# A linear-attention scan and its feed-forward on one Trainium2 core: the last eight chunks' feed-forward in pairs, two chunks' transposes back on TensorE

## The chip, the cores and the metric

The kernel runs on one core of a Trainium2 chip. The core has five engines that run beside each other and wait for one another by semaphores: TensorE (PE; its weight loads are shown as PEld), VectorE (DVE), ScalarE (ACT), GpSimd (POOL) and SyncE (SP), whose queue issues nearly all DMA transfers here. The metric is the device time of one execution in microseconds (us).

## What is computed

The first part is a recurrence per batch and head over 768 tokens, with a state of 48 x 48; the second is a feed-forward on all 3072 tokens.

```
# r, k, v, w: (4, 8, 768, 48);  u: (8, 48)
for t in range(768):
    y[t]  = r[t] @ (state + outer(u * k[t], v[t]))
    state = w[t][:, None] * state + outer(k[t], v[t])
x   = y of all heads side by side        # (3072, 384)
h   = x @ w_in                           # (384, 2048)
out = maximum(0.01 * h, h) @ w_out       # (2048, 384), float32
```

## The kernel before

**Chunks.** The 3072 tokens are cut into 24 chunks of 128 (six to a batch entry). Chunks 0 to 3 are handled in two interleaved pairs (`pair`, line 491), chunks 4 to 23 one by one (`single`, line 668). For a chunk, w, k, r and v are loaded by four DMAs (line 470; 192-byte pieces in single chunks). ACT takes the logarithm of w (line 332), PE makes the running sum over tokens with a triangular matrix (cp, line 691), ACT's exponentials (line 342) and DVE's products (line 348) make the scaled r and k, both in the tile rk. rk has to be transposed to rkT (`turn`, line 376) for the score matmuls (line 750); DVE masks the scores (line 412); PE sums state part and score part into yp (lines 780 and 785); DVE adds the bonus term and leaves y (line 444). y is transposed into xT, which holds the feed-forward's input of all tokens (`finish`, line 439). PE, DVE and POOL carry the state to the next chunk (lines 761, 434 and 421).

**Two ways to transpose.** For the chunks in `TDMA` (line 150), one DMA transpose on SP's queue makes rkT (line 381) and one makes the chunk's columns of xT (line 450). For the others, PE does eight 128 x 128 transposes of rk into the PSUM banks se and so (line 391), which DVE (line 399) and ACT (line 401) copy to rkT, and three of y into the bank yp (line 458), which ACT copies to xT (line 465). `TDMA` begins at chunk 12.

**Feed-forward.** `blocks` (line 158) says how many chunks make a block: one each. The up-projection of a block (line 821) goes in items: an item fills one PSUM bank hp of 512 columns, which with a block of one chunk are four tiles of d_ff by 128 tokens, three matmuls each (384 = 3 x 128), so 12 matmuls of 128 columns. A Prelu on ACT (line 855) takes the bank to g. The down-projection goes per chunk in four items of four matmuls of 384 columns into a bank op (line 873); the sum is copied out by ACT (line 885) or, from chunk 14 on, DVE (line 889), and an SP DMA writes it (line 893). There are two hp banks, two op banks and three g tiles. The up items of block n are interleaved in proportion with the down items of block n - 1 (lines 834 to 845), and each up item depends on the xT of all chunks of its block:

```
m1.append((up, j, J, N, g, chs, [xt_steps[ch] for ch in chs] + win_s[j * 128 // 512]))
```

**Order.** No instruction is issued while the steps are described. Each step names its engine, a guessed duration, its dependences and a priority; `Plan.order` (line 37) simulates the engines with these guesses and emits every engine's instructions in the simulated order of start. Each engine then runs its queue strictly in that order, waiting where it has to. Priorities: scan steps by chunk (10 per chunk), feed-forward items behind all of them (1000 and up), Prelu and output copies ahead (5 and 3). A DMA's guessed share of the transfer time is its `wire`: `WIRE` (line 155) for each of a single chunk's four loads, 1.7 for an rkT transpose, 0.65 for an xT transpose; transfers queue one behind the other in the simulation. Two limits keep the scan from running far ahead: the loads of chunk n depend on the running sum of chunk n - 5 (`AHEAD`), and the logarithm of chunk n on the first up item of chunk n - 8 (`LEAD`, line 899).

Of the kernel before, what the change touches and what calls it, by code (L numbers as in the profile page):

```python
# [123 lines left out]
def kernel(  # L124
# [15 lines left out]
    NCH = B * C  # L140
# [6 lines left out]
    NQ = FF // 512  # L147
    OACT = 14
    NCI = 3
    TDMA = range(12, NCH)  # L150
    LEAD = 8
    AHEAD = 5

    PAIRS = (0, 2)
    PWIRE, WIRE = 1.45, 1.15
    WEIGHTS = [(2, 20.15)] + [(4, 24.0)] * 7
    CASTS = 3
    blocks = [1] * NCH
    assert sum(blocks) == NCH

    pool = ctx.enter_context(tc.tile_pool(name="pool", bufs=1))
# [49 lines left out]
    with tc.manual_schedule():  # L211
# [51 lines left out]
        def step(eng, dur, fn, pri, reads=(), writes=(), deps=(), wire=None, rows=0):  # L263

            d = list(deps)
            for x in writes:
                d += x.old
            i = plan.add(eng, dur, fn, d, pri, wire, rows)
            for x in (*reads, *writes):
                x.steps.append(i)  # L270
            return i
# [104 lines left out]
        def turn(rk, rkT, s_d, n, P0, banks):  # L376

            if n in TDMA:
                return [step(
# [59 lines left out]
        def finish(yp, vs, s_y, s_vs, n, P0):  # L439
# [6 lines left out]
            col = n * L  # L446
            if n in TDMA:
                xt_steps.append(step(
# [483 lines left out]
```

## Time and profile before

| | us |
|---|---|
| time, median of 3 runs (lowest to highest) | 188.97 (188.82 to 189.43) |
| the profiled execution: its time | 188.97 |
| its span, first to last instruction | 187.3 |
| PE busy | 174.0 |
| DVE, ACT, POOL busy | 128.0, 116.3, 108.7 |
| PE: 1152 up matmuls (line 821), mean of one | 0.219 |
| PE: 384 down matmuls (line 873), mean of one | 0.326 |
| ACT: 96 Prelus of 512 columns (line 855), mean of one | 0.597 |
| DMA transpose to rkT (12), to xT (12), median to landing | 3.5, 2.6 |
| one single-chunk load of 192 KB, median to landing | 3.6 to 3.9 |

The span is shorter than the time; the difference lies around the first and last instruction. Matmuls overlap in the array, so a matmul's own duration (0.219 us) is longer than the distance from its start to the next one's; for what PE can do in a time, the distance of starts counts. "Idle before" an engine's instruction is the time in which the engine did nothing, and the profile names whose semaphore ended it. The DMA rows give the share of the core's 16 DMA engines.

### The profile page before, as it was taken

The page shows a single profiled execution, that of the slowest core. Times are in us where ns is not written, and L with a number is a line of the kernel's source. Part 1 is how long each engine was busy: PE and PEld are TensorE (multiplying, and loading weights), DVE is VectorE, ACT ScalarE, POOL GpSimd, SP SyncE. Part 2 cuts the span into 40 slices and gives each one's busy share as a digit, 9 for nine tenths or more (in the row PEclk, how much of TensorE's full clock was granted, in tenths as well). Part 3 has the DMA queues.
Part 4 walks back from the last instruction along what each step waited for, and adds up shares of the span by engine and source line. Part 5 has one row for each costly group of instructions (what it writes and reads, how often), then busy time and mean ns, then how long its engine had stood idle before and what let it go on. Part 6 is the DMA issues. An engine that isn't in the chain of part 4 may idle for free.

```text
span 187.3 us, 6219 instructions
## 1 busy us (share of the span) xinstructions
PE 174.0 (93%) x2550; PEld 136.1 (73%) x2550; DVE 128.0 (68%) x226; ACT 116.3 (62%) x254; POOL 108.7 (58%) x148
## 2 busy tenths in 40 slices
PE   3678579999999999999999999999999999999992
PEld 1255567688778878788787787878887877877871
DVE  2399784887789787877967999766876856441111
ACT  2646586678876877796687666676374645334430
POOL 7799922175899898978792885170545755400000
PEclk9999999999999999999999999999999999999999
DMA  5999999889899997987899879997789996512102
GB/s 147 261 316 322 385 370 302 156 189 217 164 221 211 185 221 158 221 193 172 174 207 190 156 155 229 119 200 141 159 180 179 191 202 142 123 44 67 38 7 84
DMA packets 116383, 34.62 MB, mean 185 GB/s; under 512 B 109697, under 2 KB 114818, under 8 KB 116354
## 3 DMA queue, kind: packets, MB, share of 16 engines
q1 hardware_dynamic: 116352, 34.22, 82.9%
q8 instruction: 20, 0.33, 0.7%
q14 instruction: 9, 0.07, 0.1%
q10 hardware_dynamic: 2, 0.00, 0.0%
HBM read 25.17 MB, written 4.72 MB: 160 GB/s over the span
## 4 chain that ended last, share of the span: by engine, by line
PE 81%; SPq 7%; DMA 6%; issue 1%; POOL 1%; DVE 1%; POOLq 0%; DVEq 0%
PE op L873 33%; PE hp L821 32%; DMA in<-in_moe_w_out_dram 6%; SPq L470 4%; PE se L750 3%; SPq L290 3%; PE yp L785 2%; PE cp L691 2%; PE yp L761 2%; PE yp L780 1%; PE so L391 1%; PE se L391 1%; PE yp L458 1%; PE cp L696 1%; PE yp L654 1%
## 5 line engine op out<-in xcount | busy, mean ns | idle before, releaser
L855 ACT ACTIVATE g<-hp 128x512 bf16<-128x512 f32 x96 | 57.1, 597 | 42.3 <-PE hp L821 41.4
L821 PE MATMUL hp<-xT,w_in_b 128*128 128x128 bf16 x1152 | 79.0, 219 | 0.3 <-DVE rkT L399 0.3
L873 PE MATMUL op<-w_out_b,g 128*128 128x384 bf16 x384 | 76.5, 326 | 0.8 <-DVE w_out_b L313 0.8
L821 PEld LDWEIGHTS <-w_in_b 128*128 128x128 bf16 x1152 | 69.3, 98 | 7.2 <-DVE w_in_b L313 0.2
L873 PEld LDWEIGHTS <-g 128*128 128x128 bf16 x384 | 33.0, 97 | 15.6 <-issue 0.9
L357 POOL TENSOR_TENSOR ru<-in,ub 128x384 f32<-128x384 f32 x24 | 26.9, 1119 | 19.7 <-DMA in<-in_r_dram 19.7
L369 POOL TENSOR_TENSOR vs<-in,dg 128x384 f32<-128x384 f32 x24 | 20.2, 843 | 14.7 <-DVE dg L365 11.0
L361 POOL TENSOR_TENSOR ru<-ru,in 128x384 f32<-128x384 f32 x24 | 25.7, 1072 | 0.9
L348 DVE TENSOR_TENSOR rk<-in,er 128x384 bf16<-128x384 f32 x24 | 18.2, 757 | 7.4 <-DMA in<-in_r_dram 5.5
L348 DVE TENSOR_TENSOR rk<-in,ek 128x384 bf16<-128x384 f32 x24 | 22.0, 919 | 1.4 <-ACT a L738 0.9
L421 POOL TENSOR_TENSOR sb<-s,a 128x384 bf16<-128x384 f32 x17 | 16.1, 947 | 10.7 <-DVE s L434 10.1
L412 DVE TENSOR_TENSOR m<-se,maskb 128x512 bf16<-128x512 f32 x20 | 13.8, 689 | 7.3 <-PE so L750 7.1
L444 DVE TENSOR_TENSOR y<-yp,vs 128x384 bf16<-128x384 f32 x24 | 13.3, 553 | 7.5 <-PE yp L785 5.1
L889 DVE COPY o<-op 128x384 f32<-128x384 f32 x10 | 5.6, 558 | 18.2 <-PE op L873 18.1
L337 POOL CAST vb<-in 128x384 bf16<-128x384 f32 x24 | 14.6, 614 | 4.5 <-DMA in<-in_v_dram 4.5
L332 ACT ACTIVATE lw<-in 128x384 bf16<-128x384 f32 x24 | 12.4, 520 | 3.9 <-DMA in<-in_w_dram 3.8
L365 DVE TENSOR_REDUCE dg<-ru 128x8 f32<-128x384 f32 x24 | 13.0, 543 | 1.9 <-POOL ru L361 1.8
L412 DVE TENSOR_TENSOR m<-so,maskb 128x512 bf16<-128x512 f32 x20 | 13.6, 680 | 0.0
L342 ACT ACTIVATE er<-cp 128x384 f32<-128x384 f32 x22 | 10.8, 492 | 3.5 <-DVE ci L716 3.0
L716 DVE TENSOR_TENSOR ci<-cp,lw 128x384 f32<-128x384 f32 x20 | 11.0, 549 | 1.8 <-ACT g L855 0.9
L342 ACT ACTIVATE ek<-ci 128x384 f32<-128x384 f32 x20 | 10.5, 526 | 0.0
L391 PEld LDWEIGHTS <-rk 128*128 128x128 bf16 x96 | 6.7, 103 | 5.0 <-DVE rk L348 4.2
(103 smaller groups left out, 191.0 us busy)
## 6 DMA issues: line engine op xcount, KB each, us to landing
out_dram<-o SPq DMA_DIRECT2D x24, 192.0 KB, 2.5
in<-in_w_dram SPq DMA_DIRECT2D x20, 192.0 KB, 3.6
in<-in_k_dram SPq DMA_DIRECT2D x20, 192.0 KB, 3.8
in<-in_r_dram SPq DMA_DIRECT2D x20, 192.0 KB, 3.9
in<-in_v_dram SPq DMA_DIRECT2D x20, 192.0 KB, 3.8
in<-in_moe_w_in_dram SPq DMA_DIRECT2D x4, 768.0 KB, 8.5
in<-in_moe_w_out_dram SPq DMA_DIRECT2D x4, 768.0 KB, 12.6
in<-in_w_dram SPq DMA_DIRECT2D x2, 384.0 KB, 5.0
```

The lines of the kernel that those rows point to most:

```text
L337: "POOL", 0.57, lambda: nc.gpsimd.tensor_copy(out=vb.t[:], in_=vn.t),
L342: "ACT", 0.5, lambda: nc.scalar.activation(out=out.t[:], in_=i, func=AF.Exp, scale=scale),
L348: lambda: nc.vector.tensor_tensor(out=rk.t[:, a, :, 0:D], in0=xn.t, in1=e.t[:], op=ALU.mult),
L357: lambda: nc.gpsimd.tensor_tensor(out=ru.t[:], in0=rn.t, in1=ubv, op=ALU.mult),
L361: lambda: nc.gpsimd.tensor_tensor(out=ru.t[:], in0=ru.t[:], in1=kn.t, op=ALU.mult),
L369: lambda: nc.gpsimd.tensor_tensor(out=vs.t[:], in0=vn.t, in1=dg.t[:].unsqueeze(2).to_broadcast([128, H, D]), op=ALU.mult),
L412: lambda par=par: nc.vector.tensor_tensor(out=m.t[:, par], in0=gt(sc[par].t), in1=mask.unsqueeze(1).to_broadcast([128, NP, 128]), op=ALU.m ...
L421: lambda: nc.gpsimd.tensor_tensor(out=sb.t[:].rearrange("p g a d -> p (g a) d"), in0=s_in.t[:].rearrange("p g a d -> p (g a) d"), in1=a_ap ...
L444: lambda: nc.vector.tensor_tensor(out=y.t[:], in0=hd(yp.t[:, 0:DM]), in1=vs.t[:], op=ALU.add),
L821: nc.tensor.matmul(hp.t[:, a * N : (a + 1) * N], lhsT=w_in_b[:, t, (j + a) * 128 : (j + a + 1) * 128], rhs=xT[:, t, c0 : c0 + N], start=(a ...
L855: lambda hp=hp, g=g, j=j, J=J, N=N: nc.scalar.activation(out=g.t[:, j : j + J, 0:N], in_=hp.t[:, 0 : J * N].rearrange("p (a n) -> p a n", ...
L873: nc.tensor.matmul(op.t[:, 0:DM], lhsT=g.t[:, j, off : off + 128], rhs=w_out_b[:, j, :], start=(j == 0), stop=(j == NJ - 1))
```

## The change

Chunks 12 and 13 are taken out of `TDMA`, so their rk and y are transposed on PE and copied by DVE and ACT as those of the chunks before; DMA transposes begin with chunk 14. The last eight chunks' feed-forward is done in four blocks of two chunks: an up item then fills its hp bank with two d_ff tiles by 256 tokens, six matmuls of 256 columns. A block has eight up items and eight down items. All g tiles become twice as wide (`max(blocks) * L`). The planner's guess for a single-chunk load goes from 1.15 to 1.18.

```diff
-    TDMA = range(12, NCH)
+    TDMA = range(14, NCH)
     LEAD = 8
     AHEAD = 5
 
     PAIRS = (0, 2)
-    PWIRE, WIRE = 1.45, 1.15
+    PWIRE, WIRE = 1.45, 1.18
     WEIGHTS = [(2, 20.15)] + [(4, 24.0)] * 7
     CASTS = 3
-    blocks = [1] * NCH
+    blocks = [1] * 16 + [2] * 4
```

## The prediction

> **What bounds the kernel now.** I first read the page's busy shares and slices.
>
> ```profile
> PE 174.0 (93%) x2550; PEld 136.1 (73%) x2550; DVE 128.0 (68%) x226; ACT 116.3 (62%) x254; POOL 108.7 (58%) x148
> ...
> PE   3678579999999999999999999999999999999992
> ...
> PEclk9999999999999999999999999999999999999999
> DMA  5999999889899997987899879997789996512102
> ```
>
> TensorE (PE) is full in every slice (4.7 us each) from the seventh to the last but one, at full granted clock; its idle time lies in the first 28 us. The DMA engines are nearly as full up to the 33rd slice, so two suspects remain. To choose between them I ask for the windows (length, then busy time of PE, PEld, DVE, ACT and POOL, clock, DMA share):
>
> ```profile
> 27.00:130.00 103.00, 102.69 (x1577) 82.08 (x1577) 81.46 (x140) 75.79 (x173) 69.40 (x78) 1.00 0.94 192
> 130.00:180.00 50.00, 49.94 (x682) 39.87 (x679) 26.89 (x46) 24.68 (x51) 18.21 (x21) 1.00 0.60 129
> ```
>
> and for the waits of PE from 27.3 us to the end, which hold a single row, ended at 27.31:
>
> ```profile
> PE op L873 <- DVE w_out_b L313: 0.8, 1, 0.8
> ```
>
> A busy PE may hide small gaps under overlapping matmuls, so I also took the starts of consecutive matmuls: the largest delay beyond the usual pitch after 27.3 us, apart from the changes between 128-row and 48-row matmuls, is 0.23 us at 144.4. From 27.3 to the last matmul PE is one dense queue; the time is startup, plus the sum of PE's pitches, plus the tail (copy of 0.56 us and the last output, 183.9 to 187.3). DMA is busy but late for nobody on PE. So I price the change in pitches.
>
> **What the change adds to PE.** Chunks 12 and 13 get their transposes back on PE: 8 of rk (line 391) and 3 of y (line 458) each. A chunk that has them now (start, duration, instruction):
>
> ```profile
> 79.20 0.39 PE L391 MATMUL se<-ident,rk 128*128 128x128 bf16 x4
> 79.42 0.39 PE L391 MATMUL so<-ident,rk 128*128 128x128 bf16 x4
> 79.65 0.83 PE L821 MATMUL hp<-xT,w_in_b 128*128 128x128 bf16 x12
> 80.32 0.33 PE L458 MATMUL yp<-ident,y 128*128 128x128 bf16 x3
> 80.48 0.81 PE L873 MATMUL op<-w_out_b,g 128*128 128x384 bf16 x4
> ```
>
> Durations overlap; what counts is start to start: 79.20 to 79.65 is 0.45 for eight, 80.32 to 80.48 is 0.165 for three. Two chunks: 2 x (0.45 + 0.165) = **+1.23 us**. They stand in a full queue, so nothing hides them.
>
> A rule of the Trainium skill prices them higher, so row and rule are weighed. The row: 22 transposes at a pitch of 56 ns, at granted clock 1.00; the groups' mean of 227 ns is one transpose's own duration, which overlaps the next. "TensorE: Matmul & The Clock Gate", Part 4, puts a PE transpose at about 275 ns in a kernel's context and says that full clock does not engage for it. At 275 ns the 22 would be an estimated 6 us; the pitch of the trace is used.
>
> **What it takes from PE.** The up-projections of chunks 16 to 23 are now 8 x 48 = 384 matmuls of 128 columns; they become 192 of 256. An item of 12 starts at 79.65 and its successor at 80.32: 0.67, so 55.8 ns each. The down-projection's four of 384 columns take 0.65, so 162.5 each. The line through the two gives 109.2 ns for 256 columns. An item, now 6 matmuls, goes from 0.670 to 0.655, and 32 items save **0.47 us**. The trace has no matmul of 256 columns, so bounds: two of 128, 111.6 (saving nothing), and one of 384 less one of 128, 106.7 (192 x 4.9 ns = 0.94 us). I take the line, because the small matmuls lie near it too (96 columns 42.5, 48 columns 25).
>
> The same page's section "Back-to-back issue gap" speaks of 81 ns at 128 columns and 131 at 512 in a stream with weight loads. Interpolated (98 at 256) that would be an estimated 12 us saved. The trace has its 128-column matmuls, each with its own weight load, at 55.8 ns, so that gain isn't there to take.
>
> Net on PE: 1.23 - 0.47 = **+0.76**, bounds +0.29 to +1.23.
>
> **What moves off the path.** SP loses four DMA transposes (lines 381 and 450: 3.5 and 2.6 us to landing by median, 1.2 to 1.9 us each on SP's queue between 92 and 111 us). The loads, outputs and transposes queued behind them there come sooner. Their 256-byte packets are a sixth of the queue's packet time: 25.2 us of all 16 engines for 24 transposes, so 4.2 us for these four. PE waits for none of it now, so the gain is nothing by itself; it is time gained for the scan of the later chunks. ACT gets two rkT copies of 0.59 and two xT copies of 0.48 (2.1 us), DVE two copies of 0.42. They lie in 90 to 115 us, where ACT is 65 to 75% and DVE 80 to 87% busy; their cover is the lead of xT over the up-projection, below. Without cover the full 3.0 us could show. POOL is untouched. The transposes bring waits to PE's queue: for DVE's rk products and for y, with ups and downs queued behind; ten chunks pay them now, and after 27.3 us all of these together left 0.2 us (one wait of the weight load of line 391 for rk). For two more chunks I take nothing; above, 0.2 us.
>
> ACT's Prelu keeps 96 instructions of 512 elements (0.60). Ups and downs alternate one to one in both versions except where a pair's 8 ups follow a single chunk's 4 downs: 8 x 0.655 + 4 x 0.65 of PE, plus scan work, against 8 x 0.60 of ACT, which fits. The last PE work, DVE's copy and the output DMA keep their sizes, so the tail stays.
>
> WIRE (1.15 to 1.18) changes the planner's guess for single-chunk loads only. The first of these, chunk 4's, issues at 22.43 us behind all weight loads, so the startup before it is planned as now. From there the four engine queues may be ordered anew; at the median this costs nothing, because PE finds ready work whichever comes first. Bounds: 1.7 us of gaps at 23.7 to 27.3 that might fill, and the lead of chunk 4's xT, only 0.5 us, that might be lost.
>
> **The wait that the change adds.** A pair's first up now needs the second chunk's xT as well. I counted up items (four of 12 to a chunk) and set their start beside xT's issue on SP:
>
> ```profile
> 131.69 2.25 SPq L450 DMA_TRANSPOSE xT<-y  x1
> ...
> 168.73 1.74 SPq L450 DMA_TRANSPOSE xT<-y  x1
> ```
>
> These are chunks 17 and 23. With 2.6 us to landing they arrive at 134.3 and 171.3 (their own landings: 133.9 and 171.6). Chunk 16's ups start at 132.93 and chunk 22's at 170.53: 1.0 too early for a pair, each time. Chunks 19 and 21 land 4.5 us before and level with the ups of 18 and 20. On PE, behind a waiting up stand downs and the whole scan; ACT and DVE follow. Against a stall: PE reaches these ups about 1 us later after the change, the scan gains up to 4.2 us of DMA time, and downs of the block before can go first (0.65 us each, if the planner sees the lateness). So I price it at nothing in the forecast. Uncovered it costs 1.0 + 1.0 = 2.1 us.
>
> **The sum.** The profiled execution took 188.97 us with a span of 187.3 (1.7 around it), and is itself the median of the three runs. 188.97 + 0.76 = **189.7 us**; a measurement tells about 0.3% (0.57 us) from no change, so "slower" begins at 189.54.
>
> **Rivals.**
> - The pair starves. If the planner's picture of the DMA is rosier than the chip, the first up of (16,17) and of (22,23) sits at the head of PE's queue until xT lands: up to 2.1 us more, 191.8; half of it, 190.8. It decides from the point where chunk 17 lands less than one item before the ups of 16. For it: the 1.0 us deficits. Against it: the DMA time freed, a whole chunk's worth.
> - The width buys nothing: a 256-column matmul costs two of 128, and only the transposes show: 190.2. Against it: four column counts on one line.
> - The startup gaps fill (the other side). If the new order from 22.4 us puts ready ups into the gaps at 23.7 to 27.3, up to 1.7 us come back: 189.7 - 1.7 = 188.0; half of it, 188.9. It decides only if over 0.76 us is filled. Against it: the last gap ends with the w_out cast after its landing at 26.4, which no WIRE moves.
> - Relief of the DMA shortens the whole. For it: DMA shares of 0.9 and over. Against it: PE's empty list of waits. Its price is at most PE's 0.23 us gap, so no case of its own.
>
> **Chances.** Forecast 0.57 (its own range, from the net's bounds, 189.3 to 190.2), starving pair 0.18, no gain from width 0.10, filled gaps 0.15. Faster than 188.40: over half of the filled gaps, 0.09. Within 0.3%: the rest of that and a third of the forecast, 0.06 + 0.19 = 0.25. Slower: 0.66. For 8 in 10 I leave out the fuller half of the gaps and the worst starving: 188.8 to 191.2.
>
> **What would show it.** Right: line 391 with 16 more and 458 with 6 more transposes on PE, four starts 0.22 apart; 192 up matmuls of 256 columns, an item of six 0.655 after its start; PE's waits after 27.3 us still nearly empty; the last matmul some 0.8 us later; xT of 17 and 23 earlier by 2 to 4 us. Wrong: a PE wait of over 0.3 us ahead of line 821 from 130 us on, ended by a landing; six wide matmuls in 0.67 or more, or under 0.64; a first down-projection well before or after 27.3; or a PE that ends earlier though its pitches sum to more.

## The result

Before: 188.91 us, the median of 6 runs (188.65 to 189.43). Changed: 190.11 us, the median of 6 (189.98 to 190.61). The ratio is 1.0061, with a 95% interval of 1.0042 to 1.0081: slower by 0.8 to 1.5 us. The forecast was 189.7 with a range of 188.8 to 191.2, and "slower" at 0.66. The profiled execution of the changed kernel took 189.99 us with a span of 188.2; against the 188.97 and 187.3 of before that is 1.02 and 0.9 more. In the experiments the runs of the kernel before, made beside them on the same chip, spread from 188.5 to 192 us, so a ratio there is known only to 0.3 or 0.4%; where less matters, the profiles decide.

The page's busy line and slices of the changed kernel:

```profile
PE 177.1 (94%) x2380; PEld 136.9 (73%) x2380; DVE 126.7 (67%) x228; ACT 118.4 (63%) x258; POOL 107.8 (57%) x148
...
PE   3688899999999999999999999999999999999992
...
PEclk9999999999999999999999999999999999999999
DMA  6999999988988999977988999869997773121112
```

TensorE is as full as it was. The slices of DMA are emptier in the fourth quarter, where the transfers ended earlier, and the time didn't follow them. The busy 177.1 is no measure of the change: in this execution the matmuls before 25.6 us ran at half their rate (12 ups from 23.37 to 24.65, 1.28 us and not 0.67), waiting for weights anyway, so they filled idle time. The windows from 27 us on (length, then PE, PEld, DVE, ACT, POOL, clock, DMA share):

```profile
27.00:130.00 103.00, 102.57 (x1583) 82.11 (x1581) 82.34 (x145) 77.35 (x175) 71.64 (x82) 1.00 0.91 190
130.00:180.00 50.00, 50.00 (x506) 37.77 (x504) 25.19 (x44) 25.88 (x54) 15.03 (x18) 1.00 0.54 113
```

and PE's waits from 27.3 us on:

```profile
PE op L873 <- DVE w_out_b L313: 0.2, 1, 0.2
PE so L391 <- DVE rk L348: 0.2, 1, 0.2
```

There is one new row, the wait of a transpose for rk, and none for xT ahead of line 821. The queue is still dense, so its length can be taken apart by starts. I measured each profile from the first down-projection matmul to the last matmul:

| kernel | first down | last matmul | between them | span |
|---|---|---|---|---|
| before | 27.31 | 183.53 | 156.23 | 187.3 |
| changed | 27.28 | 184.35 | 157.07 | 188.2 |

Of the 1.02 us between the two profiled executions, 0.84 lies between these two matmuls, -0.03 before them, 0.08 in the tail and 0.13 outside the span.

### The profile page after: what moved, and what is told of

It is laid out like the page before. It is cut to its first block, busy times and chain, and to the rows that moved or that the text cites. A ratio compares the mean times of both kernels' runs of the same rounds, so it can differ in the third digit from the quotient of the medians.

```text
span 188.2 us, 5870 instructions
## 1 busy us (share of the span) xinstructions
PE 177.1 (94%) x2380; PEld 136.9 (73%) x2380; DVE 126.7 (67%) x228; ACT 118.4 (63%) x258; POOL 107.8 (57%) x148
## 4 chain that ended last, share of the span: by engine, by line
PE 77%; SPq 8%; DMA 8%; DVE 2%; ACT 1%; issue 1%; ACTq 0%
PE op L873 31%; PE hp L821 31%; DMA in<-in_moe_w_out_dram 6%; SPq L470 5%; PE se L750 3%; SPq L290 3%; DMA in<-in_w_dram 2%; PE yp L785 2%; PE cp L691 2%; PE yp L761 2%; PE yp L780 1%; DVE rk L348 1%; PE so L391 1%; PE se L391 1%; PE yp L458 1%
## 5 line engine op out<-in xcount | busy, mean ns | idle before, releaser
L821 PE MATMUL hp<-xT,w_in_b 128*128 128x128 bf16 (+1 forms) x960 | 79.8, 233 | 0.0
L821 PEld LDWEIGHTS <-w_in_b 128*128 128x128 bf16 x960 | 65.4, 99 | 7.8
L873 PEld LDWEIGHTS <-g 128*128 128x128 bf16 x384 | 34.3, 98 | 16.0 <-issue 0.5
L357 POOL TENSOR_TENSOR ru<-in,ub 128x384 f32<-128x384 f32 x24 | 25.9, 1078 | 10.8 <-DMA in<-in_r_dram 10.8
L361 POOL TENSOR_TENSOR ru<-ru,in 128x384 f32<-128x384 f32 x24 | 24.7, 1029 | 1.1
L348 DVE TENSOR_TENSOR rk<-in,ek 128x384 bf16<-128x384 f32 x24 | 20.8, 868 | 1.4 <-ACT ek L342 1.3
L337 POOL CAST vb<-in 128x384 bf16<-128x384 f32 x24 | 15.6, 653 | 2.5 <-DMA in<-in_v_dram 2.5
L391 PEld LDWEIGHTS <-rk 128*128 128x128 bf16 x112 | 8.2, 107 | 4.9 <-DVE rk L348 4.3
```

The costliest lines, as they stand in the source:

```text
L337: "POOL", 0.57, lambda: nc.gpsimd.tensor_copy(out=vb.t[:], in_=vn.t),
L348: lambda: nc.vector.tensor_tensor(out=rk.t[:, a, :, 0:D], in0=xn.t, in1=e.t[:], op=ALU.mult),
L357: lambda: nc.gpsimd.tensor_tensor(out=ru.t[:], in0=rn.t, in1=ubv, op=ALU.mult),
L361: lambda: nc.gpsimd.tensor_tensor(out=ru.t[:], in0=ru.t[:], in1=kn.t, op=ALU.mult),
L821: nc.tensor.matmul(hp.t[:, a * N : (a + 1) * N], lhsT=w_in_b[:, t, (j + a) * 128 : (j + a + 1) * 128], rhs=xT[:, t, c0 : c0 + N], start=(a ...
L873: nc.tensor.matmul(op.t[:, 0:DM], lhsT=g.t[:, j, off : off + 128], rhs=w_out_b[:, j, :], start=(j == 0), stop=(j == NJ - 1))
```

## The experiments

Each kernel was executed 6 to 12 times, beside the kernel before. The table gives the timed result and the same stretch of PE's queue; the texts on record and the reading follow.

| run | median, us | ratio to before [95%] | stretch, us | against 156.23 |
|---|---|---|---|---|
| e1 transposes only | 190.55 | 1.0041 [1.0008, 1.0074] | 157.25 | +1.02 |
| e2 pairs only | 188.66 | 0.9958 [0.9924, 0.9992] | 155.48 | -0.75 |
| e3 WIRE only | 189.33 | 1.0001 [0.9968, 1.0034] | 156.38 | +0.15 |
| e4 change, WIRE 1.15 | 191.41 | 1.0098 [1.0064, 1.0131] | 158.04 | +1.81 |
| e6 no rkT transposes | 188.86 | 0.9988 [0.9967, 1.0008] | 156.22 | -0.01 |
| e7 six pairs | 191.86 | 1.0129 [1.0087, 1.0171] | 159.29 | +3.06 |
| e8 pairs, DMA from 11 | 189.19 | 0.9997 [0.9968, 1.0026] | 155.59 | -0.64 |
| e9 doubled again | 190.55 | 1.0039 [1.0001, 1.0076] | 157.30 | +1.07 |
| e10 pairs, WIRE 1.18 | 189.63 | 0.9982 [0.9948, 1.0017] | 155.92 | -0.31 |
| e11 change, WIRE 1.21 | 189.96 | 1.0021 [0.9987, 1.0056] | 157.04 | +0.81 |
| e12 change again | 190.16 | 1.0027 [0.9995, 1.0059] | 156.98 | +0.75 |

The run e5 stands with e9. The theory was that of the prediction: from 27.3 us on TensorE's queue is dense and the time is the sum of its pitches. The rivals were that the pairs starve, that freed DMA time counts, and that the new order of the queues makes the difference.

### The parts alone: e1, e2, e3, e4

```diff
 e1:  TDMA = range(14, NCH)
 e2:  blocks = [1] * 16 + [2] * 4
 e3:  PWIRE, WIRE = 1.45, 1.18
 e4:  TDMA = range(14, NCH);  blocks = [1] * 16 + [2] * 4   # WIRE stays 1.15
```

> Only the transposes of chunks 12 and 13 go back to TensorE; blocks stay at one chunk, WIRE stays 1.15. Theory of the dense queue (the time is startup plus the sum of TensorE's start-to-start pitches plus tail): 22 transposes more, 188.9 + 1.23 = 190.1 us, and TensorE's waits after 27.3 us stay under 0.5 us. Rival, the DMA time set free is worth something by itself: under 189.5. Rival, the loss of the change comes from the pairs' wait for xT: 188.9, since there are no pairs here.

> Only the last eight chunks' feed-forward in pairs; DMA transposes from chunk 12, WIRE 1.15. Theory of the dense queue: 32 items at 0.655 in place of 0.670, 188.9 - 0.47 = 188.4 us if the planner fills the time until the second chunk's xT with other work. Rival, the pair starves without the DMA time that the full change frees: waits of TensorE ahead of the first up item of chunks 16 and 22 of about 1.0 us each, 188.4 + 2.1 = 190.5. Rival, the wide matmul saves nothing: 188.9.

> Only the planner's guess for a single-chunk load goes from 1.15 to 1.18: the same work in another order. Theory of the dense queue: 188.9 us, within 0.3. Rival, the new order of the queues carries the part of the loss that the pitches don't explain: 189.2 to 189.5.

> The whole change but for the planner's guess, which stays 1.15. Theory of the dense queue: as the whole change, 188.9 + 0.76 = 189.7 by the pitches (the whole change measured 190.1). Rival, the order set by 1.18 costs 0.4 us: 189.7 here against 190.1 there. Rival, the order set by 1.18 is what keeps the pairs supplied: waits of over 0.5 us ahead of a pair's first up, 190.6 or more.

The transposes alone cost, with no pair in the kernel; so the loss isn't the pairs' wait, and the four DMA transposes less bring nothing back. In e1's profile the pitches after lines 391 and 458 sum to 6.48 us where before has 5.25: the 1.23 of the forecast. The 0.2 less in the stretch lies in small gaps, which differ from order to order and, as e9 shows below, from one execution to the next.

The pairs alone gain 0.53 us by the medians beside each other (0.15 to 1.4 by the interval), where 0.47 was expected, and they do so with the DMA as loaded as before. Their stretch is 0.75 shorter, more than the pitches give, because two gaps of before's profile (0.23 and 0.16) are absent and only one of 0.20 is new. Six wide matmuls take an item's time as forecast; in the changed kernel (start, duration, instruction):

```profile
172.79 0.82 PE L821 MATMUL hp<-xT,w_in_b 128*128 128x256 bf16 x6
173.44 0.81 PE L873 MATMUL op<-w_out_b,g 128*128 128x384 bf16 x4
174.09 0.82 PE L821 MATMUL hp<-xT,w_in_b 128*128 128x256 bf16 x6
174.75 0.33 PE L873 MATMUL op<-w_out_b,g 128*128 128x384 bf16 x1
```

From 172.79 to 173.44 is 0.65, and the pitch of one is 109 ns. WIRE alone changes nothing that can be measured. But in e4, with the old WIRE, the change is 1.3 us slower still than as it was made (0.97 of it in the stretch). Its PE queue ahead of the first pair, the 48-row score matmuls left out:

```profile
137.35 0.82 PE L873 MATMUL op<-w_out_b,g 128*128 128x384 bf16 x4
138.01 0.36 PE L785 MATMUL yp<-vb,m 128*128 128x48 bf16 x8
138.71 0.32 PE L691 MATMUL cp<-lw,trev 128*128 128x384 bf16 x1 [0.33 <-ACT a L738]
...
139.29 0.33 PE L761 MATMUL yp<-vb,rk 128*128 128x96 bf16 x4 [0.18 <-DVE y L444]
...
140.35 0.33 PE L780 MATMUL yp<-sb,rkT 128*128 128x96 bf16 x4
140.51 0.36 PE L785 MATMUL yp<-vb,m 128*128 128x48 bf16 x8
140.72 1.47 PE L821 MATMUL hp<-xT,w_in_b 128*128 128x256 bf16 x12
```

The downs of chunk 15 have run out at 138.0; until the pair's first up at 140.72 only scan steps are left, each waiting for another engine. Four gaps of 0.49, 0.32, 0.28 and 0.24 us add up to 1.33. The waits carry the names of ACT and DVE, but what is missing is ready feed-forward work: chunk 17's xT landed at 139.5. The last two gaps, 0.5 us, come after that landing; there the pair's ups were ready but stood behind scan steps in the queue, so that part is the order's and not the DMA's. The same stretch of the changed kernel has a down directly ahead of the pair:

```profile
133.59 0.83 PE L821 MATMUL hp<-xT,w_in_b 128*128 128x128 bf16 x12
134.26 0.81 PE L873 MATMUL op<-w_out_b,g 128*128 128x384 bf16 x4
134.91 0.33 PE L761 MATMUL yp<-vb,rk 128*128 128x96 bf16 x4
135.08 0.81 PE L873 MATMUL op<-w_out_b,g 128*128 128x384 bf16 x4
135.73 1.47 PE L821 MATMUL hp<-xT,w_in_b 128*128 128x256 bf16 x12
```

### The price of a transpose with the order held: e5, e9

```diff
-                    for g in range(NP):
+                    for g in [*range(NP)] * (2 if n in (8, 9) else 1):
...
-                for g in range(KT):
+                for g in [*range(KT)] * (2 if n in (8, 9) else 1):
```

> The kernel before, with each of the 22 TensorE transposes of chunks 8 and 9 issued twice into the same place. The planner's durations are untouched, so the order of every engine is that of before, no DMA is freed and the results stay the same. Theory of the dense queue: 22 pitches more, +1.23 us, 190.2 against 188.97. Rival, the transposes find slack in TensorE's queue and the loss of the change has another cause: within 0.3 of before. Rival, a transpose on TensorE costs its whole 0.23 us: +5.

> The same kernel as in the run with doubled transposes, whose profile was taken at a granted clock of 0.68 and so can't be read against before: every engine's order as in the kernel before, 22 transposes of chunks 8 and 9 issued twice. Theory of the dense queue: from the first down-projection to the last matmul 156.2 + 1.2 = 157.5 us, and 190.2 in all. Rival, slack in the queue: 156.2 and 189.0. Rival, more than the pitch is paid (a transpose holds the queue beyond 56 ns): 158 or more.

e5 came out at 1.0113 [1.0068, 1.0159] of before from four of its six executions; the profiled one took 256.87 us at a granted clock of 0.68, which makes every pitch longer, so it says slower and no more. e9 settles it by its profile. There the pitches after lines 391 and 458 sum to 6.48 us where before has 5.25, +1.23. The stretch is 1.07 longer, because two gaps of before's profile, 0.23 at 144.4 and 0.16 at 53.0, aren't there and one of 0.24 ahead of 31.4 is new. As the order is the same in both, gaps of this size come and go between executions. A chunk with its transposes doubled:

```profile
65.61 0.61 PE L391 MATMUL se<-ident,rk 128*128 128x128 bf16 x8
66.06 0.81 PE L873 MATMUL op<-w_out_b,g 128*128 128x384 bf16 x4
66.71 0.61 PE L391 MATMUL so<-ident,rk 128*128 128x128 bf16 x8
67.16 0.33 PE L458 MATMUL yp<-ident,y 128*128 128x128 bf16 x3
```

Eight take 0.45, not eight times 0.23. Same order, no DMA moved, no wide matmul: 22 transposes cost 1.23 us of queue. In e9 no copy on ACT or DVE is added, in e1 four of rkT and two of xT are, and their stretches are alike (157.30 and 157.25): the copies cost nothing that shows.

### Freed DMA time alone: e6

```diff
         def turn(rk, rkT, s_d, n, P0, banks):
+            if n in (12, 13):
+                return list(s_d)
```

> The kernel before, leaving out the rkT transposes of chunks 12 and 13 altogether, on DMA and on TensorE: their scores and state parts are computed from what an earlier chunk left in the tile. Two of the four DMA transposes that the change removes are gone, 3.1 of the 4.2 us of DMA time, and TensorE gets nothing for it. Theory of the dense queue: freed DMA time is worth nothing, 188.9, within 0.4. Rival, DMA is a bound beside TensorE: 188.4 or less.

This kernel leaves out the rkT transposes of chunks 12 and 13, so their scores come from what an earlier chunk left in the tile. The stretch is 156.22 us against 156.23, the median 188.86. With an estimated 3 us of DMA work taken out (two of the four removed transposes; the DMA queue's share of the span falls from 82.9 to 80.3%) and nothing put on PE, the time stays. The rival that DMA is a second bound falls.

### How far pairs and DMA transposes go: e7, e8, e10

```diff
 e7:  blocks = [1] * 12 + [2] * 6
 e8:  blocks = [1] * 16 + [2] * 4;  TDMA = range(11, NCH)
 e10: blocks = [1] * 16 + [2] * 4;  PWIRE, WIRE = 1.45, 1.18
```

> DMA transposes from chunk 12 and WIRE 1.15 as before, but pairs from chunk 12 on: six in place of the four of the run with pairs only. Theory of the dense queue: 48 items at 0.655 in place of 0.670, 188.97 - 0.71 = 188.3, a gain of 0.24 over four pairs. Rival, the pair starves: in the kernel before, chunk 13's xT landed 3.6 us after the start of chunk 12's ups; four downs cover 2.6 of it, so 1.0 us or more of waits around that pair and 189.3.

> Four pairs, and one chunk more transposed by DMA (from chunk 11). Theory of the dense queue: 188.97 - 0.47 - 0.61 = 187.9, under both kernels and under the pairs alone. Rival, the DMA time of one more chunk (2.1 us) makes the scan late and the pairs starve: 188.5 or more, with waits of TensorE around the first ups of the pairs.

> The pairs alone once more (DMA transposes from chunk 12), with the planner's guess at 1.18. Theory that the order decides only whether a pair is starved: 188.5 if no wait of over 0.3 us stands ahead of a pair, as in the run with pairs only; up to 191 if one does. Rival, that the pairs need the DMA time freed by the removed transposes: starved here and in any order, 189.5 or more.

e7 is the starving pair in full, and dearer than expected. The pair of chunks 12 and 13 begins at 113.76, and between 110.1 and 113.5 gaps of 1.13, 0.57, 0.48 and 0.47 us stand between scan steps. The windows around it:

```profile
108.00:112.00 4.00, 2.63 (x35) 1.51 (x32) 4.00 (x7) 1.30 (x5) 3.66 (x4) 1.00 0.69 149
112.00:116.00 4.00, 3.38 (x31) 2.36 (x29) 3.96 (x8) 1.72 (x5) 1.84 (x3) 0.65 1.20 206
116.00:120.00 4.00, 4.00 (x51) 3.26 (x50) 2.16 (x5) 3.17 (x7) 1.27 (x2) 0.93 1.07 192
...
113.30:116.50 3.20, 3.01 (x14) 2.07 (x14) 2.68 (x6) 0.74 (x2) 1.51 (x2) 0.50 1.27 184
```

The last but two column is the granted clock: PE is idle a third of the first window, and in the second the clock falls to 0.65 in the mean: it is 0.50 from 113.3 to 116.5, the window of the last row. The pair's first ups then run slowly:

```profile
113.76 3.52 PE L821 MATMUL hp<-xT,w_in_b 128*128 128x256 bf16 x18
117.12 0.33 PE L780 MATMUL yp<-sb,rkT 128*128 128x96 bf16 x4
```

Eighteen of them from 113.76 to 117.12, 3.36 us where 18 x 0.109 = 1.97 would do; the first thirteen distances of starts are 213 ns each, nearly twice 109, the last four 109. So 2.65 us of gaps cost another 1.4. The sum, -0.71 for six pairs, 2.65 and 1.4, less before's own gap of 0.23, is 3.1; measured are 3.06. The Trainium skill's page "TensorE: Matmul & The Clock Gate", Part 1, says that PE's clock falls to half after an idle window of about 3.4 us; here the half is shown, by the 0.50 and the 213 ns, but PE was only partly idle before it, by the gaps above. Which of the gaps brought it on isn't shown.

In e8 the transposes of one more chunk leave PE, 0.61 us of pitches, but the stretch is no shorter than e2's: one gap of 0.51 us ends with a landing of xT ahead of a pair at 161.1, another of 0.30 stands at 102.8 and carries the name of DVE (line 434); together they take back more than the 0.61. The first is named in PE's timeline:

```profile
161.13 0.60 PE L821 MATMUL hp<-xT,w_in_b 128*128 128x256 bf16 x4 [0.35 <-DMA xT<-y]
```

So in this order a late landing takes back most of what the fewer transposes save, though at the number of before the DMA costs nothing (e6). That the DMA sets the limit in any order isn't shown. e10 isn't told from before by its time (0.9982); its queue is 0.31 shorter, with one gap of 0.32 that ends with chunk 21's xT. The wide items take 0.655 us in it too, without the freed DMA time, so the rival that pairs need that time falls.

### The change with another order: e11, e12

```diff
 e11: PWIRE, WIRE = 1.45, 1.21     # the rest as changed
 e12: the changed kernel itself
```

> The whole change with the planner's guess at 1.21 in place of 1.18 (1.15 gave 191.4, with 1.35 us of gaps ahead of the first pair). Theory of the dense queue: 189.7 to 190.1 if the order leaves no gap ahead of a pair, and that plus the gaps if it does; it can't be less. Rival, 1.18 itself costs the 0.3 to 0.4 us by which the change exceeds the forecast: 189.7 or less with a full queue.

> The changed kernel itself, timed again beside the others of this call. By the pitches 0.76 us above before; by the first measurement 1.2 (interval 0.8 to 1.5). Within 0.2 of the doubled transposes less 0.47 if the sum of the pitches is all.

Both are as full as the first profile of the change: stretches of 157.04 and 156.98. By its time e12 isn't told from before (1.0027 [0.9995, 1.0059]); the profile tells it. e11's largest gap is 0.32 at 140.8, elsewhere than in the order of 1.18 but of much the same size. So the excess over the forecast isn't peculiar to 1.18, within the 0.2 by which the medians differ. The medians of e12 and e9 differ by 0.39, their stretches by 0.32, where the pairs should give 0.47.

The best version found is e2, pairs without the move of the transposes: 0.9958 of before [0.9924, 0.9992], and the only one whose interval lies below before, by a hair: the same work in e10's order isn't told from before.

## Why the prediction was right, step by step

**What bounds the kernel** held. The queue of PE is dense from 27.3 us in every profile but for the gaps named above, e6 shows that DMA time is worth nothing there, and e9 that a pitch added is a pitch paid.

**What the change adds: 1.23.** In the changed kernel's profile the pitches after lines 391 and 458 sum to 6.47 us against 5.25, +1.22. The duration of 0.23 us per transpose would have given 5.

**What it takes: 0.47.** The 256-column matmul came out at 109 ns, on the line between 128 and 384 columns, and e2 gained 0.53 by the medians. Neither bound was reached.

**The waits of the transposes, taken as nothing and at most 0.2,** is the term that was mis-sized. Here it is in the changed kernel:

```profile
90.07 0.81 PE L873 MATMUL op<-w_out_b,g 128*128 128x384 bf16 x4
91.07 0.40 PE L391 MATMUL so<-ident,rk 128*128 128x128 bf16 x4 [0.19 <-DVE rk L348]
91.30 0.50 PE L821 MATMUL hp<-xT,w_in_b 128*128 128x128 bf16 x6
```

Four downs from 90.07 end their pitches at 90.72; the transposes of chunk 12 start at 91.07, 0.35 later, when DVE's second product of rk is done. The two products took 1.22 and 1.35 us there, against 0.77 and 0.87 in the mean. What ran beside them on POOL:

```profile
88.33 1.00 POOL L361 TENSOR_TENSOR ru<-ru,in 128x384 f32<-128x384 f32 x1
88.52 1.22 DVE L348 TENSOR_TENSOR rk<-in,er 128x384 bf16<-128x384 f32 x1
89.29 1.31 POOL L357 TENSOR_TENSOR ru<-in,ub 128x384 f32<-128x384 f32 x1
89.66 1.35 DVE L348 TENSOR_TENSOR rk<-in,ek 128x384 bf16<-128x384 f32 x1
```

(Rows of two engines, set in order of time.) Each product ends 0.41 us after the POOL instruction that was running when it began; the products with no POOL instruction beside them took 0.54 to 0.56 us in this profile and in before's. So it looks as if each waited for POOL's; no experiment tests that. The gap is in e12's profile too (0.35, ending at 91.08), and in none of e1, e4 and e11, which move the same transposes in other orders, so it belongs to this order.

Three more gaps count. Before's profile has two that the changed kernel lacks, 0.23 at 144.4 and 0.16 at 53.0, the latter also ahead of transposes of rk; the changed kernel's has one of 0.20 ahead of a down-projection at 31.3 (0.12 in e12). The sum of the stretch is 1.22 - 0.47 + 0.35 + 0.20 - 0.23 - 0.16 = 0.91, and 0.83 for e12; measured are 0.84 and 0.75, so under 0.1 is left over. Set against the 0.16 of before, the transposes' waits grew by 0.19; those of the two moved chunks are 0.35, where at most 0.2 was allowed.

**What is left.** With 0.08 in the tail and 0.13 outside the span, the profiled executions differ by 1.02. The medians differ by 1.20; the last 0.2 is no more than the spread of before's runs, and no run tells it apart.

**The starving pair** didn't come, but my reasons for that were only half right. I expected xT of chunks 17 and 23 to be 2 to 4 us earlier for the freed DMA time. Chunk 23's was issued at 165.15, not 168.73. Chunk 17's landed at 134.9, hardly earlier than before: issued at 129.87, not 131.69, it took 5.0 us to land, with two rkT transposes issued right behind it. My landing of 133.9 for before was a misreading: that is where SP's row of the issue ends (131.69 + 2.25), and the transfer's packets ran until 134.5. The first pair's deficit was therefore at least 1.5 us, not 1.0. What covered the first pair was order: the downs of chunk 15 run ahead of it, and its ups start at 135.73, not 132.93, behind an xT that had landed 0.8 us before. I hadn't worked out that order, so in this the forecast was lucky: with 1.15 for WIRE the time, 191.41, lies above its range. e2 shows that pairs need no freed DMA time. e4 shows that they can starve with it, at 1.33 us, between the half and the full price that the prediction gave; e7 shows a price that I hadn't foreseen, the clock.

**WIRE** costs nothing by itself (e3), as forecast. That it decides whether the pairs are supplied was in the prediction only as "if the planner sees the lateness". The startup gaps didn't fill: the first down-projection is at 27.28 us.

## What to carry to other kernels

When an engine's queue is dense, price a change in that queue by distances of starts, not by durations, and take a wider matmul from the line through its neighbours; work taken off a busy engine that nobody waits for is worth nothing, until some new dependence needs its result earlier. When blocks are made wider, ask what ready work stands ahead of the first one: a hole there costs its length, and in e7, with 2.65 us of holes in 3.4, the clock fell as well. A change made of two parts should be priced in two parts: here one gained and the other cost more.

## What was not expected of the hardware

Gaps that left PE idle for 2.65 of 3.4 us, with short matmuls between them, were followed by a granted clock of 0.50 from 113.3 to 116.5, and half as much again was lost as in the gaps themselves (e7). The startup ran at half rate in some executions (12 ups in 1.28 us at 23 us in the changed kernel, 0.67 in before), while the first down-projection came at 27.25 to 27.86 us in every profile; in most of them the wait named there is that for the cast of w_out. DVE's products of rk took 0.54 to 0.56 us with nothing on POOL beside them and up to 1.36 with it.
